# Attention and two routed MLPs: the first block of the second MLP stage gates its last rows on TensorE alone, and the block's steps stand in another order

## The chip, the cores and the metric

The kernel runs on one core of a Trainium2 chip. TensorE (PE) multiplies matrices and transposes tiles; VectorE (DVE), ScalarE (ACT) and GpSimd (POOL) work element by element; SyncE (SP), ACT and POOL issue transfers. The metric is the device time of one launch in microseconds (us).

## What is computed

Inputs: q, k, v of 4 batches x 8 heads x 576 positions x 64, and the weights of two expert stages with N = 2304 rows, D = 512, E = 8 experts, F = 1024.

```python
x = attention_with_rope(q, k, v)                  # 2304 x 512
# first expert stage
logits = x @ w_gate + modality_bias[modality_id]
e = argmax(logits); g = softmax(logits)[e]
x = g * (relu(x @ w1[e]) @ w2[e])
# second expert stage
out = x.copy()
rows = x @ w_skip > 0
e = argmax(x[rows] @ w_gate2); g = softmax(x[rows] @ w_gate2)[e]
out[rows] = x[rows] + g * (relu(x[rows] @ w1_2[e]) @ w2_2[e])
```

## The kernel before

Attention runs first, then the first expert stage (`moe1`) in blocks of 256 rows, each of one expert, then the second (`moe2`) in blocks of 128 rows. Rows get to their expert through lists in DRAM: a row's gate is worked out, its place in its expert's list counted, its number and gate value scattered to the list by an indirect DMA of POOL (`list<-tgs,si`, one issue for 128 rows); a block loads its list, gathers its rows (`xh<-out_dram,tok`), computes, and scatters the result (`out_dram<-x,tok`).

Matrix products work on fp32 values split in a high and a low part, three products for each. ACT casts the high parts of weights and activations (L1000 for w1, L1013 for w2, L1097 for x, L1452 for the hidden rows hT), and DVE subtracts for the low parts (L1004, L1016, L1101, L1453). Blocks 0 to 3 of the second stage belong to the expert with the most rows; on this input ten blocks (0 to 9) run, and during blocks 3 to 8 the weights of the next block's expert are split: four pieces of w1 and eight chunks of w2.

A block of the second stage (`body(i)` in `moe2`) consists of these steps: `mm1(hf, ...)` multiplies the rows with half hf of w1 (L1434), 12 matmuls for a half; `relu(hf)` on ACT (L1444) takes the result out of PSUM; `h_tr(hf)` transposes it on PE (L1449) and splits it into hT (ACT L1452, then DVE L1453); `mm2` multiplies hT with w2 (L1474), 24 matmuls; `xt(i + 1)` turns and splits the next block's rows (L1094, L1097, L1101); `split1` and `split2` split weights for the next block. At the end DVE makes the result (L1532) and POOL scatters it. Every engine works its own instructions off in the order in which the code writes them, so the order of steps in `body` is the order in each queue; `mm1` of the next block needs xT and the w1 pieces, `mm2` needs hT and the w2 chunks.

What is still to be done for the first stage's last 256 rows (its tiles t = 0 and t = 1 of 128 rows) stands in block 0 of the second stage, as calls `last(t, stage)`: `out` scales the rows out of PSUM on ACT (L1183, into tile `x20` or `x21`); the second gate's nine columns (eight experts and the skip score) are then worked out; `top` takes the best expert; `count` and `list` find the place and scatter the list entry. The gate has two ways. For t = 0 before, POOL multiplies x20 with three gate columns (`prod`, L1190, in `moe1`), ACT sums them (`sums`, L1195) and DVE multiplies and sums the six others (L1199). For t = 1, `turn` transposes the rows on PE (L1206), copies them to SBUF on ACT (L1208) and scatters the rows to `out`; `gate` is four matmuls with nine columns (L1213). The tiles `x20` and `x21` are also the source of scatters by POOL's queue. The `prod` tiles are two buffers of `x2t` and the tile `prod`; `relu` and `turn` take their result tiles from the same pool `x2t`.

The functions in the listing keep the line numbers of the profile.

Of the kernel before, what the change touches and what calls it, by code (L numbers as in the profile page):

```python
# [112 lines left out]
class Kernel:  # L113
# [1016 lines left out]
    def moe1(self):  # L1130
# [37 lines left out]
        def epi(i, t, stage):  # L1168
# [5 lines left out]
            if stage == "meta":  # L1174
# [3 lines left out]
                    s[name] = self.rot(f"{name}_{t}", [128, w], dt, bufs=1)  # L1178
                nc.scalar.copy(s["tg"], l[:, t])
                nc.scalar.copy(s["ti"], l[:, t, 0:1])  # L1180
            elif stage == "out":
                s["x2"] = self.rot(f"x2{t}", [128, DM], bufs=1)
                nc.scalar.activation(s["x2"], s["y"], AF.Copy, scale=s["tg"][:, 1:2])  # L1183
            elif stage == "prod":


                s["prod"] = [self.rot("x2t", [128, 4, 128]).rearrange("p c t -> p (c t)") for _ in range(3)][0:2]
                s["prod"].append(self.rot("prod", [128, DM], bufs=1))
                for j, w in enumerate(s["prod"]):
                    nc.gpsimd.tensor_tensor(w, s["x2"], self.gw[j], op=ALU.mult)  # L1190
                    if j == 0:
                        self.scatter(self.out, s["ti"], s["x2"], N)
            elif stage == "sums":
                for j, w in enumerate(s["prod"]):
                    nc.scalar.activation(w, w, AF.Copy, accum_out=s["lg"][:, j : j + 1])  # L1195
            elif isinstance(stage, tuple):

                for e in stage:
                    nc.vector.scalar_tensor_tensor(  # L1199
                        self.junk, s["y"], s["tg"][:, 1:2], self.gw[e], op0=ALU.mult, op1=ALU.mult, accum_out=s["lg"][:, e : e + 1]  # L1200
                    )
            elif stage == "turn":
                x2 = s["x2"]
                ps = self.bank("T")
                for dc in range(4):
                    nc.tensor.transpose(ps[:, dc * 128 : dc * 128 + 128], x2[:, dc * 128 : dc * 128 + 128], self.ident)  # L1206
                s["x2t"] = self.rot("x2t", [128, 4, 128], F32)
                nc.scalar.copy(s["x2t"].rearrange("p c t -> p (c t)"), ps)  # L1208
                self.scatter(self.out, s["ti"], x2, N)
            elif stage == "gate":  # L1210
                pg = self.bank("G")
                for dc in range(4):
                    nc.tensor.matmul(pg[:, 0 : E + 1], s["x2t"][:, dc], self.wg2s[:, dc], start=dc == 0, stop=dc == 3)  # L1213
                nc.vector.tensor_copy(s["lg"], pg[:, 0 : E + 1])
            elif stage == "top":
                v = s["v"]
                lg, nm, d = s["lg"], tl_("nm", [128, 1]), tl_("d", [128, E])
                nc.vector.tensor_reduce(nm, lg[:, 0:E], axis=AX.X, op=ALU.max, negate=True)
                nc.vector.tensor_scalar(d, lg[:, 0:E], nm, None, op0=ALU.add)
                ex = tl_("ex", [128, E])  # L1220
                s["se"] = self.rot("se", [128, 1], F32, bufs=3)
                nc.scalar.activation(ex, d, AF.Exp, accum_out=s["se"])
                t8, m8 = tl_("t8", [128, E]), tl_("m8", [128, 1])
                nc.vector.scalar_tensor_tensor(t8, d, 0.0, self.w8, op0=ALU.is_equal, op1=ALU.mult)
                nc.vector.tensor_reduce(m8, t8, axis=AX.X, op=ALU.max)
                nc.vector.tensor_scalar(v[:, 0:1], s["tg"][:, 0:1], float(N), None, op0=ALU.is_lt)
                nc.vector.tensor_scalar(v[:, 1:2], lg[:, E : E + 1], 0.0, v[:, 0:1], op0=ALU.is_gt, op1=ALU.mult)
                nc.vector.tensor_tensor(m8, m8, v[:, 1:2], op=ALU.mult)
                s["oh"] = self.rot("oh", [128, E], BF16)
                nc.vector.tensor_scalar(s["oh"], self.w8, m8, None, op0=ALU.is_equal)  # L1230
            elif stage == "count":
                pr = s["pr"] = self.bank("G")
                nc.tensor.matmul(pr[:, 0:E], self.U, s["oh"], start=True, stop=False)
                nc.tensor.matmul(pr[:, 0:E], self.ones, self.acc2, start=False, stop=True)
            else:
                v, oh = s["v"], s["oh"]
                nc.vector.tensor_scalar(s["se"], s["se"], 1e-9, None, op0=ALU.add)
                tg = self.rot("tgs", [128, 2], bufs=4)
                nc.vector.reciprocal(tg[:, 1:2], s["se"])
                nc.scalar.copy(tg[:, 0:1], s["tg"][:, 0:1])  # L1240
                sl, sf, si = tl_("sl", [128, E]), tl_("sf", [128, 1]), self.rot("si", [128, 1], I32, bufs=3)
                nc.vector.tensor_tensor(sl, s["pr"][:, 0:E], self.ebase, op=ALU.add)
                nc.vector.tensor_tensor(sl, sl, oh, op=ALU.mult)
                nc.vector.tensor_tensor(self.acc2, self.acc2, oh, op=ALU.add)
                nc.vector.tensor_reduce(sf, sl, axis=AX.X, op=ALU.add)
                nc.vector.tensor_scalar(v[:, 2:3], v[:, 1:2], float(-BIG), float(BIG), op0=ALU.mult, op1=ALU.add)
                nc.vector.tensor_tensor(si, sf, v[:, 2:3], op=ALU.add)
                self.scatter(self.lists[1], si, tg, E * CAP)
                del eps[i, t]
# [159 lines left out]
    def moe2(self):  # L1409
# [14 lines left out]
        def body(i):  # L1424
# [48 lines left out]
                    for hi, wi in ((0, 0), (0, 1), (1, 0)):  # L1473
                        nc.tensor.matmul(y, hT[:, hi, f], w2s[:, wi, f], start=(f == 0 and hi + wi == 0), stop=(f == 7 and hi == 1))  # L1474

            last(1, "out")
            last(0, "sums", (3, 4, 5), (6, 7, 8))
            mm1(0, range(0, 1))
            last(1, "turn")
            if i == 0:  # L1480
                self.moe2_second()
            mm1(0, range(1, 2))
            last(0, "top")
            if i == 0:
                split2(0, range(0, 4))
            split2(i, range(4, 8))
            if i + 2 > NA2 + 1:
                self.seq_load(q, i + 2, 1)
            mm1(0, range(2, 4))
            relu(0)  # L1490
            last(0, "count", "list")
            last(1, "gate", "top")
            mm1(1, range(0, 2))
            h_tr(0)
            split1((0,))
            mm1(1, range(2, 4))
            split1((1,))
            relu(1)
            last(1, "count")
            if i > 0:  # L1500
                fetch(i + 2)
            if i + 3 > NA2:
                self.seq_list(q, i + 3)
            mm2(range(0, 2))
            last(1, "list")
            if i == 0:

                for j in range(NE2, NA2):
                    self.seq_list(q, j)
            h_tr(1)  # L1510
            split1((2, 3))
            if i + 3 > NA2 + 1:
                self.seq_load(q, i + 3, 0)
            mm2(range(2, 4))
            if i == 1:
                tot = self.counts(self.acc2, "d")
            xt(i + 1)
            mm2(range(4, 8))
            if i == 1:

# [81 lines left out]
```

## Time and profile before

| | before |
|---|---|
| median of 3 runs | 750.29 us (750.17 to 752.8) |
| profiled execution | 752.11 us |
| its span on the core | 750.5 us |
| mean granted TensorE clock | 0.979 |

The profile comes from one execution, whose own time is 752.11 us, 1.6 us over its span. Times in the rows are microseconds from the span's start. A timeline row reads: start, busy time, engine, line, operation, result<-inputs, shape, number of instructions of the group, and in brackets the engine's idle time ahead of it with what ended it. In a windows row the busy time of each engine in the stretch stands with its count of instructions.

### The profile page before, as it was taken

What the parts mean: (1) busy time and instruction counts of PE and PEld (TensorE: products, weight loads), DVE (VectorE), ACT (ScalarE), POOL (GpSimd) and SP (SyncE); (2) the same over time, 40 slices, a digit from 0 to 9 for tenths busy, and PEclk for the clock granted to TensorE, in tenths of its full rate; (3) what the DMA queues carried; (4) which work ended last, traced back from release to release, by engine and by line L of the source; (5) the groups of instructions that cost most, each with busy time, mean ns of one, the idle gap of its engine ahead of it and who ended that gap; (6) DMA issues with size and microseconds to landing.
All of it is one profiled execution on the core that took longest, in us unless ns stands there. A gap on an engine that the chain in (4) does not pass through costs nothing. (4 is left out here: it accounts for less than half of the span.)

```text
span 750.5 us, 15355 instructions
## 1 busy us (share of the span) xinstructions
PE 709.6 (95%) x4844; PEld 643.2 (86%) x4844; DVE 548.4 (73%) x1335; ACT 458.2 (61%) x1046; POOL 376.3 (50%) x464
## 2 busy tenths in 40 slices
PE   6899999999999999978999999999998969999995
PEld 6799999999999999978989988998897748777773
DVE  6789999999999999974436544655569773489892
ACT  3788888888888888881223332333255452387881
POOL 7755576759587855244244554254355312123233
PEclk9899999999999999998999999999999989999998
DMA  5665556555656554470411110110677031679910
GB/s 141 129 156 140 127 127 149 130 125 131 155 129 141 137 133 92 103 239 0 128 58 58 57 43 29 43 57 16 170 266 234 22 118 39 249 250 326 331 48 18
DMA packets 76656, 94.68 MB, mean 126 GB/s; under 512 B 29736, under 2 KB 50472, under 8 KB 76547
## 3 DMA queue, kind: packets, MB, share of 16 engines
q1 hardware_dynamic: 67970, 78.22, 37.5%
q0 software_dynamic: 7200, 12.46, 5.3%
q10 hardware_dynamic: 1376, 2.75, 1.1%
q8 instruction: 43, 0.70, 0.4%
q14 instruction: 67, 0.54, 0.3%
HBM read 64.48 MB, written 12.97 MB: 103 GB/s over the span
## 5 line engine op out<-in xcount | busy, mean ns | idle before, releaser
L430 PE MATMUL S<-w1s 128*128 128x288 f32 x640 | 134.1, 323 | 4.0 <-ACT w1s L386 1.3
L1164 PE MATMUL psY<-w2s,hT 128*128 128x512 f32 x480 | 116.0, 396 | 0.0
L1115 PE MATMUL psM<-xT,w1s 128*128 128x256 f32 x864 | 110.6, 286 | 2.6 <-DVE hT L1128 2.6
L1115 PEld LDWEIGHTS psM<-xT,w1s 128*128 128x128 f32 x864 | 106.5, 191 | 3.7 <-DVE hT L1128 3.1
L430 PEld LDWEIGHTS S<-w1s 128*128 128x128 f32 x640 | 98.7, 192 | 8.8 <-ACT PP L447 1.7
L1164 PEld LDWEIGHTS psY<-w2s,hT 128*128 128x128 f32 x480 | 87.9, 188 | 17.3
L447 ACT ACTIVATE PP<-S,nm 128x576 f32<-128x576 f32 x128 | 95.8, 749 | 6.5 <-DVE nm L443 4.4
L443 DVE TENSOR_REDUCE nm<-S 128x1 f32<-128x576 f32 x128 | 94.8, 750 | 3.8 <-PE S L430 3.7
L532 DVE TENSOR_TENSOR tl<-T,th 128x512 fp32r<-128x512 f32 x128 | 88.0, 687 | 12.7 <-ACT th L528 9.4
L525 PE MATMUL T<-ident,PP 128*128 128x128 f32 x512 | 94.3, 274 | 0.8 <-DVE w1s L399 0.4
L528 ACT CAST th<-T 128x512 fp32r<-128x512 f32 x128 | 75.1, 587 | 17.8 <-PE T L525 15.2
L559 PE MATMUL O<-th,vh 128*128 128x288 f32 x256 | 76.4, 332 | 0.9 <-ACT os L568 0.9
L525 PEld LDWEIGHTS T<-ident,PP 128*128 128x128 f32 x512 | 63.9, 140 | 3.4 <-DVE tl L532 1.0
L559 PE MATMUL O<-tl,vh 128*128 128x288 f32 x256 | 64.5, 305 | 0.0
L1434 PE MATMUL psM<-w1s,xT 128*128 128x512 f32 x240 | 63.0, 408 | 1.0 <-DVEq L1351 0.7
L1474 PE MATMUL psY<-w2s,hT 128*128 128x512 f32 x240 | 62.2, 401 | 0.0
L962 POOL DMA_INDIRECT list<-tgs,si x20 | 21.5, 1076 | 80.0 <-issue 40.4
L330 POOL TENSOR_TENSOR mem_w<-qkn,mem_w 128x640 f32<-128x640 f32 x30 | 46.8, 1561 | 20.4 <-PE T L367 20.2
L1128 DVE SCALAR_TENSOR_TENSOR hT<-psM,hT 128x512 fp32r<-128x512 f32 x36 | 24.8, 688 | 43.1 <-ACT hT L1123 43.1
L1434 PEld LDWEIGHTS psM<-w1s,xT 128*128 128x128 f32 x240 | 44.7, 192 | 12.7 <-DVE xT L1101 2.2
L1183 ACT ACTIVATE x<-psY,tg 128x512 f32<-128x512 f32 x20 | 13.8, 689 | 67.7 <-PE psY L1164 56.4
L1101 DVE TENSOR_TENSOR xT<-psT,xT 128x512 fp32r<-128x512 f32 x31 | 20.4, 686 | 44.2 <-ACT xT L1097 43.1
(276 smaller groups left out, 1522.6 us busy)
## 6 DMA issues: line engine op xcount, KB each, us to landing
raw<-in_moe_w_dram SPq DMA_DIRECT2D x24, 512.0 KB
mem_w<-in_moe_w_dram SPq DMA_DIRECT2D x20, 512.0 KB
w1s<-w1s SPq DMA_DIRECT2D x30, 256.0 KB
raw1b<-in_moe_w_dram SPq DMA_DIRECT2D x12, 512.0 KB
raw2b<-in_moe_w_dram SPq DMA_DIRECT2D x12, 512.0 KB
w1s<-w1s SPq DMA_DIRECT2D x16, 288.0 KB
qkn<-in_q_dram SPq DMA_DIRECT2D x16, 256.0 KB
qkn<-in_k_dram SPq DMA_DIRECT2D x16, 256.0 KB
```

The source lines that it names most:

```text
L330: eng.tensor_tensor(r, x, tb[:, i, 0].unsqueeze(1).broadcast_to([128, 2, 5, D]), op=ALU.mult)
L430: yield nc.tensor.matmul(ps[:, hf, 0:288], s["wide"][:, o : o + 128], s["K"][h % 2][:, kk, hf * 288 : hf * 288 + 288], start=first and kk ...
L443: nc.vector.tensor_reduce(st[h // 2]["nm"][:, h % 2, c : c + 1], hs[h]["ps", c][:, :, 0:288], axis=AX.XY, op=ALU.max, negate=True)
L447: nc.scalar.activation(PP[:, c, h % 2 * S : h % 2 * S + S].rearrange("p (a b) -> p a b", a=2), hs[h]["ps", c][:, :, 0:288], AF.Exp, bias=s ...
L525: yield nc.tensor.transpose(ps[:, c * 128 : c * 128 + 128], PP[:, c, o : o + 128], ident)
L528: nc.scalar.copy(hs[h]["th"][:, j, 0:512], hs[h]["tp", j])
L532: nc.vector.tensor_tensor(s["tl"][:, j, 0:512], s["tp", j], s["th"][:, j, 0:512].bitcast(F32), op=ALU.subtract)
L559: yield nc.tensor.matmul(s["ot"][:, hf, 0:288], st[h // 2]["vh"][:, h % 2, j].rearrange("p s d -> p (s d)"), w[:, hf * 288 : hf * 288 + 28 ...
L1115: self.nc.tensor.matmul(ps[:, a], self.w1s[:, wi, dc, fs], x[:, xi, dc], start=(dc == 0 and wi + xi == 0), stop=(dc == 3 and wi == 1))
L1164: nc.tensor.matmul(ps, h[:, hi, f, t * 128 : t * 128 + 128], w2s[:, wi, f], start=(f == 0 and hi + wi == 0), stop=(f == 7 and hi == 1))
L1434: nc.tensor.matmul(ms[hf], x[:, xi, dc], w1s[:, wi, dc, hf * 512 : hf * 512 + 512], start=(dc == 0 and wi + xi == 0), stop=(dc == 3 and xi ...
L1474: nc.tensor.matmul(y, hT[:, hi, f], w2s[:, wi, f], start=(f == 0 and hi + wi == 0), stop=(f == 7 and hi == 1))
```

## The change

The last rows of t = 0 get their gate on PE too: a stage `turn only` (the transposition and the copy, without the scatter, which POOL has issued already) and `gate` take the place of the three sums on ACT and the six products on DVE. POOL's three products stay in `moe1`'s body; nothing reads them now. The rows of t = 1 are scaled into a tile of their own, `x2l`, where before it was `x21`. The steps of `body` stand in another order: in block 0, w2 is split in three parts, and gate, count and list stand elsewhere; in every block `relu(1)` and its half of `mm1` stand ahead of `split1`'s first piece, the second piece behind `h_tr(1)`, and the third and fourth, with the load of w1 that follows them, behind `xt(i + 1)`.

```diff
--- before.py
+++ after.py
@@ -1178,8 +1178,9 @@
                     s[name] = self.rot(f"{name}_{t}", [128, w], dt, bufs=1)
                 nc.scalar.copy(s["tg"], l[:, t])
                 nc.scalar.copy(s["ti"], l[:, t, 0:1])
-            elif stage == "out":
-                s["x2"] = self.rot(f"x2{t}", [128, DM], bufs=1)
+            elif stage in ("out", "last out"):
+
+                s["x2"] = self.rot(f"x2{t}" if stage == "out" else "x2l", [128, DM], bufs=1)
                 nc.scalar.activation(s["x2"], s["y"], AF.Copy, scale=s["tg"][:, 1:2])
             elif stage == "prod":
 
@@ -1199,14 +1200,15 @@
                     nc.vector.scalar_tensor_tensor(
                         self.junk, s["y"], s["tg"][:, 1:2], self.gw[e], op0=ALU.mult, op1=ALU.mult, accum_out=s["lg"][:, e : e + 1]
                     )
-            elif stage == "turn":
+            elif stage in ("turn", "turn only"):
                 x2 = s["x2"]
                 ps = self.bank("T")
                 for dc in range(4):
                     nc.tensor.transpose(ps[:, dc * 128 : dc * 128 + 128], x2[:, dc * 128 : dc * 128 + 128], self.ident)
                 s["x2t"] = self.rot("x2t", [128, 4, 128], F32)
                 nc.scalar.copy(s["x2t"].rearrange("p c t -> p (c t)"), ps)
-                self.scatter(self.out, s["ti"], x2, N)
+                if stage == "turn":
+                    self.scatter(self.out, s["ti"], x2, N)
             elif stage == "gate":
                 pg = self.bank("G")
                 for dc in range(4):
@@ -1473,48 +1475,54 @@
                     for hi, wi in ((0, 0), (0, 1), (1, 0)):
                         nc.tensor.matmul(y, hT[:, hi, f], w2s[:, wi, f], start=(f == 0 and hi + wi == 0), stop=(f == 7 and hi == 1))
 
-            last(1, "out")
-            last(0, "sums", (3, 4, 5), (6, 7, 8))
+
+            last(0, "turn only")
+            last(1, "last out")
             mm1(0, range(0, 1))
             last(1, "turn")
             if i == 0:
                 self.moe2_second()
+            last(0, "gate", "top")
             mm1(0, range(1, 2))
-            last(0, "top")
             if i == 0:
-                split2(0, range(0, 4))
-            split2(i, range(4, 8))
-            if i + 2 > NA2 + 1:
-                self.seq_load(q, i + 2, 1)
+                split2(0, range(0, 2))
+            else:
+                split2(i, range(4, 8))
+                if i + 2 > NA2 + 1:
+                    self.seq_load(q, i + 2, 1)
+            last(1, "gate", "top")
             mm1(0, range(2, 4))
             relu(0)
-            last(0, "count", "list")
-            last(1, "gate", "top")
             mm1(1, range(0, 2))
+            last(0, "count")
             h_tr(0)
+            last(0, "list")
+            mm1(1, range(2, 4))
+            relu(1)
+            if i == 0:
+                split2(0, range(2, 4))
             split1((0,))
-            mm1(1, range(2, 4))
-            split1((1,))
-            relu(1)
-            last(1, "count")
             if i > 0:
                 fetch(i + 2)
             if i + 3 > NA2:
                 self.seq_list(q, i + 3)
             mm2(range(0, 2))
+            last(1, "count")
+            h_tr(1)
+            split1((1,))
             last(1, "list")
             if i == 0:
+                split2(0, range(4, 8))
 
                 for j in range(NE2, NA2):
                     self.seq_list(q, j)
-            h_tr(1)
-            split1((2, 3))
-            if i + 3 > NA2 + 1:
-                self.seq_load(q, i + 3, 0)
             mm2(range(2, 4))
             if i == 1:
                 tot = self.counts(self.acc2, "d")
             xt(i + 1)
+            split1((2, 3))
+            if i + 3 > NA2 + 1:
+                self.seq_load(q, i + 3, 0)
             mm2(range(4, 8))
             if i == 1:
```

ACT's queue at the start of block 0, before, with what each row waits for (L1351 is the last instruction of the first stage; DMASW are the counters of POOL's indirect transfers, one for each of eight queues; names with _49 are the counters of engines):

```order
L1183 ACTIVATE x_0_5294<-psY_5149,tg_0_5203 128x512 [waits DMASW3_49,DMASW2_49,DMASW5_49,DMASW1_49,DMASW6_49,DMASW0_49,DMASW7_49,PE_49,Activation_49]
L1195 ACTIVATE x2t_5133,lg_0_5176<-x2t_5133 128x512 [waits DVE_49,Pool_49]
L1195 ACTIVATE x2t_5132,lg_0_5176<-x2t_5132 128x512 [waits Pool_49]
L1195 ACTIVATE prod_5575,lg_0_5176<-prod_5575 128x512 [waits Pool_49]
L1208 COPY x2t_5132<-psT_5183 128x512 [waits PE_49,Activation_49]
L1222 ACTIVATE e_ex_5380,se_5383<-e_d_5376 128x8 [waits DVE_49]
L1013 CAST w2s<-raw2b 128x512 [waits DMAHW6_49]
```

And of the change:

```order
L1209 COPY x2t_5132<-psT_5183 128x512 [waits DVE_49,PE_49,Pool_49]
L1184 ACTIVATE x2l_10903<-psY_5149,tg_0_5203 128x512 [waits Activation_49]
L1209 COPY x2t_5133<-psT_5182 128x512 [waits PE_49]
L1224 ACTIVATE e_ex_5380,se_5383<-e_d_5376 128x8 [waits DVE_49]
L1013 CAST w2s<-raw2b 128x512 [waits DMAHW6_49]
L1224 ACTIVATE e_ex_5381,se_5384<-e_d_5377 128x8 [waits DVE_49]
L1446 ACTIVATE x2t_5132<-psM_5307 128x512 [waits PE_49,Activation_49]
```

The scaled rows of t = 1 wait for nothing but ACT itself now, and stand behind the copy of the turned rows of t = 0, which waits for a count of POOL's.

PE's queue at the same place, before (psM is the result of mm1, psT of a transposition, psG of the gate; x_0_5294 are the rows of t = 1):

```order
L1434 MATMUL psM_5307<-w1s,xT_5124 128x512 [waits DVE_49,Activation_49]
L1434 MATMUL psM_5307<-w1s,xT_5124 128x512 [waits DVE_49]
L1434 MATMUL psM_5307<-w1s,xT_5124 128x512
L1206 MATMUL psT_5183<-ident,x_0_5294 128x128 [waits Activation_49]
L1206 MATMUL psT_5183<-ident,x_0_5294 128x128 x3
L1434 MATMUL psM_5307<-w1s,xT_5124 128x512 x9
...
L1213 MATMUL psG_5126<-wg2s,x2t_5132 128x9 [waits Activation_49]
L1213 MATMUL psG_5126<-wg2s,x2t_5132 128x9 x3
```

And of the change (x_0_5180 are the rows of t = 0):

```order
L1207 MATMUL psT_5183<-ident,x_0_5180 128x128 [waits DVE_49,Activation_49]
L1207 MATMUL psT_5183<-ident,x_0_5180 128x128 x3
L1436 MATMUL psM_5307<-w1s,xT_5124 128x512 [waits DVE_49] x2
L1436 MATMUL psM_5307<-w1s,xT_5124 128x512
L1207 MATMUL psT_5182<-ident,x2l_10903 128x128 [waits Activation_49]
L1207 MATMUL psT_5182<-ident,x2l_10903 128x128 x3
L1215 MATMUL psG_5127<-wg2s,x2t_5132 128x9 x4
L1436 MATMUL psM_5307<-w1s,xT_5124 128x512 x3
L1215 MATMUL psG_5126<-wg2s,x2t_5133 128x9 [waits DVE_49,Activation_49]
L1215 MATMUL psG_5126<-wg2s,x2t_5133 128x9 x3
```

Four transpositions and four gate matmuls have come in, and the transposition of t = 1 still stands behind the first three matmuls of mm1.

ACT's queue in a block behind which the expert changes, from relu(0) to the w2 casts, before (branches left out; raw_70 and raw2b are loaded weights):

```order
L1444 ACTIVATE x2t_5133<-psM_5307 128x512
L1452 CAST hT<-psT_5182 128x4x128
...
L1000 CAST w1s<-raw_70 128x4x256
...
L1000 CAST w1s<-raw_70 128x4x256
...
L1444 ACTIVATE x2t_5132<-psM_5308 128x512
L1452 CAST hT<-psT_5183 128x4x128
...
L1000 CAST w1s<-raw_70 128x4x256 x2
...
L1097 CAST xT_4883<-psT_5182 128x4x128
...
L1013 CAST w2s<-raw2b 128x512 x4
```

And of the change:

```order
L1446 ACTIVATE x2t_5132<-psM_5307 128x512
L1454 CAST hT<-psT_5183 128x4x128
L1446 ACTIVATE x2t_5133<-psM_5308 128x512
...
L1000 CAST w1s<-raw_70 128x4x256
...
L1454 CAST hT<-psT_5182 128x4x128
...
L1000 CAST w1s<-raw_70 128x4x256
...
L1097 CAST xT_4883<-psT_5183 128x4x128
...
L1000 CAST w1s<-raw_70 128x4x256 x2
...
L1013 CAST w2s<-raw2b 128x512 x4
```

The second relu (to x2t_5132 before, x2t_5133 now) has moved ahead of the four w1 casts, and the w1 casts stand one piece further on each: behind relu(1), behind hT of the second half, and behind xT.

## Rows read from the trace of the kernel before

**Rows 1.** The page's first part: busy time, share and instructions of PE.

```profile
PE 709.6 (95%) x4844; PEld 643.2 (86%) x4844; DVE 548.4 (73%) x1335; ACT 458.2 (61%) x1046; POOL 376.3 (50%) x464
```

**Rows 2.** Windows by block of the second stage: block 0, 2, 3 to 8, 9.

```profile
core 0: us, PE busy (x) PEld busy (x) DVE busy (x) ACT busy (x) POOL busy (x), PEclk, DMA share, GB/s
599.41:623.17 23.76, 16.42 (x76) 12.63 (x77) 15.93 (x56) 10.54 (x27) 5.90 (x6) 0.86 0.29 102
...
635.68:648.12 12.44, 12.44 (x62) 10.18 (x60) 7.11 (x26) 2.96 (x5) 1.80 (x3) 1.00 0.44 142
648.12:728.30 80.18, 76.92 (x361) 60.05 (x360) 67.46 (x87) 62.07 (x96) 22.30 (x26) 1.00 0.74 260
728.30:741.35 13.05, 12.92 (x61) 9.85 (x59) 8.16 (x14) 6.27 (x12) 4.84 (x4) 1.00 0.02 2
```

**Rows 3.** Timeline of all engines where the second stage begins.

```profile
599.41 0.93 PE L1434 MATMUL psM<-w1s,xT 128*128 128x512 f32 x3 [0.72 <-DVEq L1351]
...
600.56 1.27 POOL L1190 TENSOR_TENSOR prod<-x,raw1b 128x512 f32<-128x512 f32 x1
...
601.90 2.26 SPq L1036 DMA_DIRECT2D raw1b<-in_moe_w_dram  x4
...
604.76 0.69 ACT L1183 ACTIVATE x<-psY,tg 128x512 f32<-128x512 f32 x1 [10.50 <-DMA out_dram<-x,ti]
...
605.50 1.11 PE L1206 MATMUL psT<-ident,x 128*128 128x128 f32 x4 [5.16 <-ACT x L1183]
```

**Rows 4.** Windows of block 0, columns as in group 2.

```profile
602.00:602.25 0.25, 0.00 (x0) 0.00 (x0) 0.21 (x3) 0.00 (x0) 0.00 (x0) 0.91 0.00 0
602.25:605.50 3.25, 0.00 (x0) 0.00 (x1) 2.15 (x6) 0.74 (x2) 0.00 (x0) 0.50 0.75 252
605.50:609.00 3.50, 3.50 (x11) 2.91 (x12) 1.40 (x9) 3.48 (x11) 1.00 (x1) 0.50 0.96 345
...
614.85:616.50 1.65, 0.00 (x0) 0.00 (x0) 1.41 (x9) 1.16 (x4) 0.97 (x1) 1.00 0.02 5
```

**Rows 5.** Timeline of PE later in block 0.

```profile
609.78 1.04 PE L1213 MATMUL psG<-wg2s,x2t 128*128 128x9 f32 x8
...
616.55 0.17 PE L1233 MATMUL psG<-oh,U 128*128 128x8 bf16 x1 [1.73 <-DVE oh L1230]
```

**Rows 6.** Timeline: from block 0's lists to the rows of block 2.

```profile
615.53 0.98 POOL L962 DMA_INDIRECT list<-tgs,si  x1 [8.72 <-issue]
...
620.24 0.97 POOL L962 DMA_INDIRECT list<-tgs,si  x1 [3.73 <-DVE hT L1453]
...
624.47 1.01 POOL L962 DMA_INDIRECT out_dram<-x,tok  x1 [0.32 <-DVE x L1532]
...
628.05 1.06 POOL L952 DMA_INDIRECT xh<-out_dram,tok  x1 [2.37 <-DMA out_dram<-x,tok]
...
632.46 0.64 PE L1094 MATMUL psT<-ident,xh 128*128 128x128 f32 x4
```

**Rows 7.** DMA issues in 627 to 628.9 us: count, median us to landing.

```profile
xh<-out_dram,tok POOLq DMA_INDIRECT x1, 3.6
```

**Rows 8.** Timeline of ACT over one block in which the expert changes.

```profile
677.69 0.60 ACT L1444 ACTIVATE x2t<-psM 128x512 f32<-128x512 f32 x1 [0.25 <-PE psM L1434]
679.52 0.59 ACT L1452 CAST hT<-psT 128x512 fp32r<-128x512 f32 x1 [1.23 <-PE psT L1449]
680.26 2.00 ACT L1000 CAST w1s<-raw1b 128x1024 fp32r<-128x1024 f32 x2 [0.15 <-DMA raw<-in_moe_w_dram]
682.16 0.59 ACT L1444 ACTIVATE x2t<-psM 128x512 f32<-128x512 f32 x1
683.54 0.59 ACT L1452 CAST hT<-psT 128x512 fp32r<-128x512 f32 x1 [0.79 <-ACT x2t L1444]
...
686.66 4.26 ACT L1013 CAST w2s<-mem_w 128x512 fp32r<-128x512 f32 x8
691.07 0.60 ACT L1444 ACTIVATE x2t<-psM 128x512 f32<-128x512 f32 x1 [0.15 <-issue]
```

**Rows 9.** Timeline of PE in the same block, its only wait.

```profile
682.80 0.66 PE L1449 MATMUL psT<-ident,x2t 128*128 128x128 f32 x4 [0.56 <-ACT x2t L1444]
```

**Rows 10.** Timeline of DVE in the same block.

```profile
688.24 2.48 DVE L1016 TENSOR_TENSOR w2s<-mem_w,w2s 128x512 fp32r<-128x512 f32 x4
```

## The prediction

> **What bounds the kernel now.** I read the page first: PE is busy 95% of the span [rows 1], so the time can fall only where PE idles or runs at half clock. The windows by block show where that is in the second stage. Block 0 takes 23.76 us with 16.42 us of PE work at a mean clock of 0.86; block 2, which splits no weights, runs without a gap in 12.44; the six blocks 3 to 8, each followed by another expert's weights, take 80.18 us, 13.36 each, of which PE idles 3.26 in all; the last takes 13.05 [rows 2]. So there is something to win in block 0 (7.34 us of idle) and some 0.9 us in each of the six.
>
> The timeline of block 0 says what PE waits for. Its first three matmuls end at 600.34, and the next thing in its queue, the transposition of t = 1's scaled rows, starts at 605.50, because ACT scales them only at 604.76; ACT has idled 10.50 us by then, with a scatter of POOL's as the releaser [rows 3]. The order lists it: that scaling waits for the counters of seven of POOL's transfer queues. The windows show what this costs beside the gap: the clock leaves full speed (2.4 GHz) at about 602.2, after 1.9 us without work, and is at half (1.2 GHz) until 609.0, that is for 3.5 us after work has come back [rows 4]. A later gap, the count of t = 1 waiting 1.73 us for its one-hot row [rows 5], leaves the clock at 1.00 [rows 4].
>
> In the six blocks I read ACT's timeline: from one relu(0) to the next are 13.38 us, and what lies between is a queue with small gaps (0.25, 1.23, 0.15, 0.79, 0.15) [rows 8]. PE's one gap in the block, 0.56 us, is the transposition of the second half, which waits for relu(1); that relu stands behind two w1 casts of 2.00 us together [rows 8, 9].
>
> **Block 0: the gate of t = 0 on PE, the tile x2l.** Removed are three sums on ACT and six products on DVE; both lie in the stretch in which PE waits for something else, and are worth nothing by themselves. x2l takes the wait for the seven transfer queues away. But ACT's queue now has the copy of t = 0's turned rows ahead of it, and that copy waits for a count of POOL's. The copy writes a buffer of the pool in which POOL's products lie, and these still run. The last product ends at 600.56 + 1.27 = 601.83, and SP's load into the weights' buffer goes out at 601.90 [rows 3]; I take the copy to start there too, at 601.9. The scaling follows some 0.55 later (an ACT instruction of that shape is busy 0.59 [rows 8]), and PE's transposition 0.74 behind the scaling's start (604.76 to 605.50 before), so at about 603.2: 2.3 us earlier, not 5.
>
> From there to block 1 PE had 15.49 us of work (16.42 less the first 0.93) and 2.18 of idle (7.34 less 5.16). The work grows by the gate of t = 0: its four transpositions lie in the gap and cost nothing there (0.66 of it [rows 9]); its gate costs what the gate of t = 1 shows, 1.04 busy, 0.89 until the next matmul starts [rows 5]. Of the idle, the 1.73 goes, since the count of t = 1 now stands behind the first chunks of mm2 with its top worked out long before; I leave 0.45 for relu and the w2 splits, which are late by turns. Does the clock still fall? PE idles from about 600.95 to 603.2, 2.25 us: longer than the 1.9 after which it fell and the 1.73 through which it stayed. So I take half clock, for 3.5 us as before. Block 1 then starts at 603.2 + 15.49 + 0.89 + 0.45 = 620.0 instead of 623.17: **-3.2**. Bounds: if the clock stays up, the 3.5 us at half [rows 4] shrink by at most 1.75, of which I take 1.2, as part of the stretch is waiting: -4.4; if all 2.18 us of idle come back in another place (the w2 chunks now arrive in three lots, and each lot is waited for), 621.8, -1.4.
>
> The Trainium skill ("TensorE: Matmul & The Clock Gate", section "Wait — 56ns, not 53.3ns?") has a floor of about 25 ns from start to start for small matmuls. By it the eight recorded gate matmuls would take 0.2 us in place of the 0.89 measured here, and the sum would be 0.7 lower; the row disagrees, and it decides.
>
> **What comes early because of it: block 2's rows.** Block 2's rows are gathered on POOL behind a chain: list scatter of t = 0 at 615.53, of t = 1 at 620.24 (4.71 later), loads of lists, the scatter of block 0's result at 624.47, the gather at 628.05 [rows 6], which lands 3.6 us later [rows 7], at 631.65. PE takes the rows at 632.46 [rows 6], 0.8 us after. If block 1 starts 3.2 earlier, PE wants them at 629.3. The list of t = 0 stands on DVE behind hT's low part, and I put its scatter at 614.0, 1.5 earlier; with 4.71 to t = 1 and everything else behind it as before, the gather lands at about 630.1. So PE waits 0 to 0.85; I take **+0.6**, near the upper end, since the intervals are measured ones.
>
> The Trainium skill ("DMA: Bandwidth & Descriptors", section "Anatomy of one DMA — SWDGE (gpsimd) path") gives a fixed 2.0 us for a transfer of this kind; if the second list followed the first by that, the gather would be in time and the sum 0.6 lower. The row shows 4.71 between the two.
>
> **Blocks 3 to 9: relu(1) ahead of the w1 casts.** It takes away what PE waits for at the second transposition, but moves 4 us of w1 casts to later places in ACT's queue, where they push the w2 casts, and behind these the next block's relu(0). I follow ACT's queue with the durations of [rows 8], from relu(0) at 0. hT of the first half starts at 1.3 (if PE waits for the relu) to 1.8 (as before, 677.69 to 679.52). relu(1) needs six more matmuls and ends at 3.3 to 3.7. Then a w1 cast (to 4.3 to 4.7), hT of the second half, which waits for PE's transposition behind six matmuls of mm2 (to 5.3 to 5.9), the second w1 cast (to 6.4 to 6.9), xT, which waits for six more matmuls and a transposition (to 7.1 to 7.7), the last two w1 casts (to 9.2 to 9.6), the eight w2 casts of 4.26 (to 13.5 to 13.9), and relu(0) again. The gap that the w1 casts filled, ahead of relu(1), is now empty; that is why the round gets no shorter though a wait of PE's is gone. DVE decides between the ends: its w2 low parts, 2.48 for four [rows 10], stand ahead of the low part of hT, for which mm2 waits. It is busy 67.46 of 80.18 us [rows 2], so I take the upper, 13.9.
>
> Block 3 has no w2 casts ahead of its own relu(0), and wins: 12.6, near the 12.44 of block 2. Blocks 4 to 8 take 13.9 each. Block 9 splits nothing but begins behind the last w2 casts: 13.05 and the 0.6 by which its relu(0) is later, 13.7. Together 12.6 + 69.5 + 13.7 = 95.8 against 80.18 + 13.05 = 93.23: **+2.6**. Bounds: with 13.5 a block, 12.44 + 67.5 + 13.05 = 93.0, -0.2; with another 0.5 a block from DVE, 14.4, it is 12.6 + 72.0 + 14.1 = 98.7, +5.5. The load of w1 that moved behind the last two casts waits for their buffer anyway; that its weights come in time I take from the casts, which wait 0.15 us at most in their idle for a transfer [rows 8].
>
> **Sum.** -3.2 + 0.6 + 2.6 = 0.0. The profiled execution took 752.11 us, 1.6 over its span of 750.5, and would take that again; it lies 1.8 above the median of 750.29, and I put the change on the median: **750.3 us**. A measurement of this kernel can tell about 0.5%, 3.75 us, from no change.
>
> **Rivals.**
> 1. Faster: nothing new is waited for in the six blocks. relu(1) ahead of the casts takes PE's idle of 3.26 us away and relu(0) is not pushed, because the casts catch up in ACT's idle (2.6 us a block in [rows 8]). With -3.2 in block 0, and the gather in time, that is -6.5: 743.8. For it: ACT is busy only 62.07 of 80.18 us [rows 2]. Against it: those gaps are ACT waiting for PE at places that stay.
> 2. Slower: the low parts on DVE become the bound. hT's low part waits behind w2's eight low parts, mm2 behind it, and the next casts behind mm2's transpositions; a round then takes about 14.6. 12.6 + 73.0 + 14.3 = 99.9, +6.7, with -3.2 and 0.6 in all +4.1: 754.4. It decides from about 14.5 a block on. For it: DVE has only 2.1 us a block to spare. Against it: the w1 low parts come later now, not earlier, and DVE's work has not grown.
> 3. The change doesn't do what it says: the count that the copy waits for comes not with POOL's product but only when POOL has waited for its own transfers, near 604.4, just ahead of where ACT began before (604.76). Then the copy stands ahead of the scaling for nothing, block 0 gains only the 1.73 less the gate's 0.89 and some of the sums, about 1, and the time is 752.5.
>
> **How the numbers follow.** Forecast 0.58, rival 1 0.17, rival 2 0.13, rival 3 0.12. Rival 3 and the forecast lie within 0.5%: faster 0.17, same 0.70, slower 0.13. The forecast with its bounds (-4.4 to -1.4, 0 to 0.85, -0.2 to +5.5) spans 746 to 755 at the extremes, seldom together; leaving out most of rival 1 and half of rival 2 gives a range of 745.5 to 754.5.
>
> **What would show it.** In block 0: ACT's copy at about 601.9 and the transposition of x2l at 603.2 (604.5 or later is rival 3), the clock at 0.50 for some 3.5 us behind it, block 1's first matmul at 620, and PE waiting for a gather at block 2's xt. In blocks 4 to 8: no PE gap at the second transposition, but one at the first, waiting for a relu(0) that stands behind w2 casts, and 13.9 us from relu(0) to relu(0). The forecast is wrong if that round is under 13.4, or if the matmuls of mm2 wait for low parts of hT by more than a few tenths.

## The result and the profile after

The changed kernel took 757.2 us (median of 4 runs, 756.49 to 758.07) beside 751.54 for the kernel before on the same chip: a ratio of 1.0078, 95% interval 1.0056 to 1.01. It is slower, and the prediction's 750.3 us, with its range to 754.5, is missed. A longer comparison (12 runs beside 28 of before, below) gave 1.0041, 1.0024 to 1.0058.

The windows by block of the changed kernel: block 0, block 1, blocks 3 to 8, block 9, with the columns of [rows 2].

```profile
600.24:623.58 23.34, 20.09 (x88) 16.30 (x89) 11.89 (x45) 9.53 (x22) 5.72 (x5) 0.78 0.30 104
623.58:637.10 13.52, 12.71 (x62) 10.21 (x61) 3.91 (x10) 3.12 (x6) 4.62 (x7) 1.00 0.17 56
649.54:731.28 81.74, 77.14 (x361) 60.35 (x360) 66.33 (x87) 62.15 (x94) 27.82 (x26) 1.00 0.70 254
731.28:745.37 14.09, 13.11 (x61) 9.85 (x59) 9.19 (x14) 7.19 (x14) 4.84 (x4) 1.00 0.02 2
```

Block 1 of before, which stands between the first two rows of [rows 2]:

```profile
623.17:635.68 12.51, 12.51 (x62) 10.13 (x61) 3.89 (x10) 3.13 (x6) 4.09 (x7) 1.00 0.18 59
```

Block 0 takes 23.34 us where it took 23.76, block 1 13.52 where it took 12.51, the six blocks 81.74 where they took 80.18, the last 14.09 where it took 13.05. So block 0 gave 0.4 us, block 1 took 1.0, and blocks 3 to 9 took 2.6 (95.83 against 93.23).

The timeline at the start of the second stage answers to [rows 3], all of it 0.83 us later in this execution.

```profile
601.42 1.27 POOL L1191 TENSOR_TENSOR prod<-x,raw1b 128x512 f32<-128x512 f32 x1
...
602.77 0.58 ACT L1209 COPY x2t<-psT 128x512 f32<-128x512 f32 x1 [7.64 <-POOLq L1353]
603.25 0.69 ACT L1184 ACTIVATE x2l<-psY,tg 128x512 f32<-128x512 f32 x1
603.99 1.11 PE L1207 MATMUL psT<-ident,x2l 128*128 128x128 f32 x4 [2.43 <-ACT x2l L1184]
604.90 1.71 PE L1215 MATMUL psG<-wg2s,x2t 128*128 128x9 f32 x8
...
609.45 4.64 PE L1436 MATMUL psM<-w1s,xT 128*128 128x512 f32 x12
...
633.84 0.66 PE L1094 MATMUL psT<-ident,xh 128*128 128x128 f32 x4 [0.81 <-DMA xh<-out_dram,tok]
```

The copy starts as POOL's last product ends, and the transposition of t = 1's rows follows 1.2 us behind it, at 603.99: 2.3 us earlier than before, counted from the stage's start. But eight gate rows take 1.71 instead of 1.04 [rows 5], and twelve matmuls of mm1 take 4.64. The last row is block 2's rows: PE waits 0.81 for their gather. The clock (the first figure behind POOL's busy time) in windows of the same stretch, for [rows 4]:

```profile
602.50:602.75 0.25, 0.00 (x0) 0.00 (x0) 0.00 (x0) 0.00 (x0) 0.18 (x1) 0.98 0.00 0
602.75:603.99 1.24, 0.00 (x0) 0.00 (x0) 0.00 (x0) 1.17 (x2) 0.00 (x0) 0.50 0.39 40
603.99:612.75 8.76, 8.76 (x31) 7.79 (x32) 4.45 (x20) 2.50 (x8) 1.00 (x1) 0.50 0.64 237
612.75:613.00 0.25, 0.25 (x2) 0.17 (x1) 0.00 (x0) 0.25 (x1) 0.00 (x0) 0.54 0.00 0
```

Work comes back at 603.99, and the clock is at half until about 613.0, 9.0 us later. Before, it was back at full 3.5 us after the work.

In the later blocks, ACT from one relu(0) to the next, for [rows 8]:

```profile
680.10 0.58 ACT L1446 ACTIVATE x2t<-psM 128x512 f32<-128x512 f32 x1
681.48 0.59 ACT L1454 CAST hT<-psT 128x512 fp32r<-128x512 f32 x1 [0.79 <-ACT x2t L1446]
682.89 0.60 ACT L1446 ACTIVATE x2t<-psM 128x512 f32<-128x512 f32 x1 [0.82 <-PE psM L1436]
683.63 1.05 ACT L1000 CAST w1s<-raw1b 128x1024 fp32r<-128x1024 f32 x1
685.32 0.59 ACT L1454 CAST hT<-psT 128x512 fp32r<-128x512 f32 x1 [0.64 <-PE psT L1451]
686.29 1.05 ACT L1000 CAST w1s<-raw1b 128x1024 fp32r<-128x1024 f32 x1 [0.38 <-DMA raw2b<-in_moe_w_dram]
687.25 0.58 ACT L1097 CAST xT<-psT 128x512 fp32r<-128x512 f32 x1
687.84 2.00 ACT L1000 CAST w1s<-raw1b 128x1024 fp32r<-128x1024 f32 x2
689.74 4.26 ACT L1013 CAST w2s<-mem_w 128x512 fp32r<-128x512 f32 x8
693.91 0.58 ACT L1446 ACTIVATE x2t<-psM 128x512 f32<-128x512 f32 x1
```

The round takes 13.81 us here (13.38 before). ACT now waits 0.82 ahead of relu(1), where two casts stood, 0.64 ahead of the second hT, and the last two w1 casts run only behind xT; w2's casts follow, and relu(0) behind them. PE feels it at the first transposition and in mm2:

```profile
694.55 0.66 PE L1451 MATMUL psT<-ident,x2t 128*128 128x128 f32 x4 [0.52 <-ACT x2t L1446]
...
697.65 1.19 PE L1476 MATMUL psY<-w2s,hT 128*128 128x512 f32 x4 [0.58 <-DVE hT L1455]
```

and DVE's rows name the second wait: four low parts of w2 stand ahead of the low part of hT.

```profile
694.51 2.48 DVE L1016 TENSOR_TENSOR w2s<-mem_w,w2s 128x512 fp32r<-128x512 f32 x4
696.92 0.67 DVE L1455 TENSOR_TENSOR hT<-psT,hT 128x512 fp32r<-128x512 f32 x1
```

### The profile page after: what moved, and what is told of

It reads as the page before. It is cut to its first block, busy times and chain, and to the rows that moved or that the text cites. A ratio compares the mean times of both kernels' runs of the same rounds, so it can differ in the third digit from the quotient of the medians.

```text
span 754.8 us, 15358 instructions
## 1 busy us (share of the span) xinstructions
PE 715.0 (95%) x4856; PEld 648.2 (86%) x4856; DVE 544.2 (72%) x1324; ACT 458.3 (61%) x1041; POOL 381.3 (51%) x464
## 3 DMA queue, kind: packets, MB, share of 16 engines
q10 hardware_dynamic: 1376, 2.75, 1.1%
## 5 line engine op out<-in xcount | busy, mean ns | idle before, releaser
L1164 PE MATMUL psY<-w2s,hT 128*128 128x512 f32 x480 | 116.1, 396 | 0.0
L1164 PEld LDWEIGHTS psY<-w2s,hT 128*128 128x128 f32 x480 | 87.9, 188 | 17.3
L447 ACT ACTIVATE PP<-S,nm 128x576 f32<-128x576 f32 x128 | 95.8, 749 | 6.5 <-DVE nm L443 4.4
L532 DVE TENSOR_TENSOR tl<-T,th 128x512 fp32r<-128x512 f32 x128 | 88.0, 687 | 12.7 <-ACT th L528 9.1
L1476 PE MATMUL psY<-w2s,hT 128*128 128x512 f32 x240 | 63.9, 403 | 3.2 <-DVE hT L1455 1.9
L330 POOL TENSOR_TENSOR mem_w<-qkn,mem_w 128x640 f32<-128x640 f32 x30 | 46.9, 1563 | 20.6 <-PE T L367 20.4
L1476 PEld LDWEIGHTS psY<-w2s,hT 128*128 128x128 f32 x240 | 43.1, 188 | 14.4 <-DVE hT L1455 4.1
L1436 PEld LDWEIGHTS psM<-w1s,xT 128*128 128x128 f32 x240 | 45.8, 195 | 10.1
L334 POOL TENSOR_TENSOR mem_w<-qkn,mem_w 128x320 f32<-128x320 f32 x60 | 51.0, 873 | 0.0
```

Of the source, the lines that this page charges most:

```text
L334: eng.tensor_tensor(t2r[:, :, :, a : a + 32], x[:, :, :, o : o + 32], sn, op=ALU.mult)
L447: nc.scalar.activation(PP[:, c, h % 2 * S : h % 2 * S + S].rearrange("p (a b) -> p a b", a=2), hs[h]["ps", c][:, :, 0:288], AF.Exp, bias=s ...
L532: nc.vector.tensor_tensor(s["tl"][:, j, 0:512], s["tp", j], s["th"][:, j, 0:512].bitcast(F32), op=ALU.subtract)
L1164: nc.tensor.matmul(ps, h[:, hi, f, t * 128 : t * 128 + 128], w2s[:, wi, f], start=(f == 0 and hi + wi == 0), stop=(f == 7 and hi == 1))
L1436: nc.tensor.matmul(ms[hf], x[:, xi, dc], w1s[:, wi, dc, hf * 512 : hf * 512 + 512], start=(dc == 0 and wi + xi == 0), stop=(dc == 3 and xi ...
```

## The experiments

Ratios are to the kernel before, run on the same chip; "blocks" are read from each kernel's own profile.

**1. The steps of before in blocks 1 to 9.** Block 0 stays changed.

```diff
             last(0, "list")
+            if i > 0:
+                split1((0,))
             mm1(1, range(2, 4))
+            if i > 0:
+                split1((1,))
             relu(1)
...
             h_tr(1)
-            split1((1,))
+            if i == 0:
+                split1((1,))
+            else:
+                split1((2, 3))
...
```

> The changed kernel with the steps of blocks 1 to 9 in the order of before; block 0 stays changed. If the new place of the w1 casts is what costs in blocks 3 to 9 (95.8 us there in the changed kernel against 93.2), these blocks come back to about 93.2 and the time falls by 2.6 us against the changed kernel, to about 0.4% over before. Rival: the later blocks are slow because block 0 hands them its lists and rows late, whatever their own order: then they stay at 95 to 96 and the time does not move.

1.001 (0.999 to 1.003). Blocks 3 to 9 took 94.0 us, of which PE waits 0.95 for one late gather in block 7; without it they are at before's 93.2. So the order in these blocks is what costs there, not the early block 0. Block 0, the same instructions as in the changed kernel, took 22.25, with 6.8 us at half clock where the changed kernel's profile has 10.2. The windows in which the clock falls and comes back:

```profile
598.50:598.75 0.25, 0.25 (x4) 0.25 (x3) 0.00 (x0) 0.25 (x1) 0.00 (x0) 0.78 1.09 377
605.25:605.50 0.25, 0.25 (x2) 0.15 (x2) 0.00 (x0) 0.23 (x1) 0.00 (x0) 0.57 0.04 16
```

Work had come back at 597.66, so the clock fell 1.0 us after it, and was back at full 7.8 us after it.

**2. Block 0 of before, the new order of relu(1) and the casts.**

> The other half alone: block 0 with the gate, the tile and the steps of before, relu(1) ahead of the casts in all blocks. If the two parts add, block 0 takes 23.8, block 1 12.5 with no wait for the gather, blocks 3 to 9 95.8: 2.6 us over before (0.35%). Rival: the two parts touch, and without the early block 0 the later blocks lose less or more than 2.6.

1.004 (1.0021 to 1.0059), 3.0 us; block 0 23.73, block 1 12.51 without a wait, blocks 3 to 9 95.74. By the blocks the parts add: +0.4 in run 1 and +2.5 here, against +3.2 for the whole change.

**3. The gates behind the first half of mm1.**

```diff
-            last(0, "gate", "top")
             mm1(0, range(1, 2))
...
-            last(1, "gate", "top")
             mm1(0, range(2, 4))
+            last(0, "gate", "top")
             relu(0)
+            last(1, "gate", "top")
```

> The changed kernel with both gates moved behind the first half of mm1, so that after the transposition of t = 1 nine matmuls of mm1 follow one another, as before. If the small gate matmuls between them kept the clock at half for 9.0 us, it is back some 3.5 us after that transposition, and block 0 takes 20.5 to 21.5 us in place of 23.3. Rival: the half clock has the same length whatever stands there, or block 0's time is set by the three lots of w2 chunks: block 0 stays within 0.5 of 23.3.

Block 0 and the clock in it:

```profile
597.74:618.01 20.27, 17.24 (x88) 13.81 (x89) 11.75 (x45) 9.43 (x22) 5.60 (x5) 0.92 0.35 119
601.29:604.00 2.71, 2.71 (x9) 2.32 (x10) 0.43 (x1) 1.56 (x3) 0.03 (x1) 0.50 0.90 328
604.00:604.25 0.25, 0.25 (x2) 0.24 (x1) 0.25 (x2) 0.06 (x1) 0.25 (x1) 0.63 0.65 262
```

With work from 601.29 on and no gate amid it, the clock is back at 604.2, 2.9 us later, and block 0 takes 20.27 us: 3.1 under the changed kernel, and what the prediction had put on block 0 (620.0 less 599.41, 20.6). The three lots of w2 chunks are the same in both. One profile shows this. The mean granted clock of the whole span, which does not say where the clock fell, fits it in the other executions: it is 0.983 to 0.985 in eight of this run's twelve, and at most 0.981 in the twelve of run 5, the changed kernel. (6.8 us less at half clock, of 750, would raise that mean by 0.0045, an estimate.)

The whole time does not show the gain as clearly: it ran at 1.0036 (1.0013 to 1.0059), 2.7 us over before, where the profile's blocks give +0.2 (block 0 -3.5, block 1 +1.0, blocks 3 to 9 +2.7). The interval reaches down to +1.0. Three executions have a mean clock of 0.975 and take 754 to 756 us; what executions differ by elsewhere is told at the end.

**4. x2l ahead of the copy on ACT.**

```diff
-            last(0, "turn only")
             last(1, "last out")
+            last(0, "turn only")
```

> The changed kernel with one step turned round: ACT scales the rows of t = 1 ahead of the copy that waits for POOL. PE's gap then shrinks from 2.4 to about 1.2 us, the clock should stay at full, and the gates and matmuls run at full: block 0 about 18 to 19 us in place of 23.3. The list chain on POOL does not shorten by as much, so block 2's gather should be waited for by some 3 us, and of the 5 won 2 to 3 should stay. Rival: the clock falls all the same, and block 0 gains only the 1.2 us of the gap.

0.9991 (0.9972 to 1.001), block 0 in 18.00 us with no half clock, block 1 in 13.04. PE waits 0.32 for block 2's gather, not the 3 that were expected, because the first list scatter came earlier too: 12.1 us into block 0, where it was 16.1 before. On PE the gates now cost what [rows 5] had:

```profile
598.51 0.60 PE L1207 MATMUL psT<-ident,x2l 128*128 128x128 f32 x4
600.08 1.06 PE L1215 MATMUL psG<-wg2s,x2t 128*128 128x9 f32 x8 [0.96 <-ACT x2t L1209]
600.99 0.95 PE L1436 MATMUL psM<-w1s,xT 128*128 128x512 f32 x3
601.77 0.96 PE L1215 MATMUL psG<-wg2s,x2t 128*128 128x9 f32 x8
```

The gap is now 0.96, ahead of the gate. Against the changed kernel (run 5, 1.0041) the ratios show 3.7 of the 5.3 us won in block 0.

**5. The changed kernel again.**

> The changed kernel itself once more. The blocks of the first two profiles account for 3.2 us over before (block 0 -0.4, block 1 +1.0, blocks 3 to 9 +2.6), while the medians of four runs stood 5.7 apart. If the blocks tell the whole effect, a longer comparison gives about 3 us over before (0.4%), and block 0 a half clock of 6.8 to 10.2 us, as its two profiles so far; if the change also costs something outside these blocks, the difference stays at 5 to 6 us (0.7%).

1.0041 (1.0024 to 1.0058), 3.1 us over before: the 3.2 of the first profile's blocks are the whole effect. Block 0 took 23.65 with 10.2 us at half clock, blocks 3 to 9 96.1.

**6. The first w1 piece back ahead of relu(1).**

> The changed kernel with one step put back: the first w1 piece ahead of the second half of mm1 and so of relu(1); the other three pieces stay late. If blocks 4 to 8 are slow because ACT stands empty ahead of relu(1) and makes up for it behind xT, the cast fills that gap again and a round takes 12.9 to 13.3 us instead of 13.6 to 14.1: 3 to 5 us less. Rival: the round is set by DVE, hT's low part behind the w2 low parts (mm2 waits 0.34 for it in each block): then it stays at 13.6 or more.

A miss: 1.0035 (1.0019 to 1.0051), rounds of 13.6 to 14.1 as in the changed kernel, blocks 3 to 9 95.8. ACT has no gap ahead of relu(1) any more, and waits 1.57 us ahead of the second hT instead. "The gap ahead of relu(1)" as the sole cause falls. The rival, a round set by hT's low part, keeps its forecast here: in each block mm2 still waits 0.34 to 0.48 us.

**7. Runs 1 and 4 together.**

> Both mends together: x2l ahead of the copy, and blocks 1 to 9 in the order of before. If the parts add, block 0 takes 18.0 us, block 1 13.0 with its wait for the gather, blocks 3 to 9 93.2 to 94.0: 4.5 to 5.2 us under before, 0.65%. Rival: an earlier block 0 only moves the wait to the gathers of the later blocks, and less than 3 us is left.

0.9952 (0.9934 to 0.997), 3.6 us under before, less than expected; block 0 18.24, block 1 13.47, blocks 3 to 9 93.15.

**8. relu(1) between the first two pieces.** As run 7, with

```diff
-            if i > 0:
-                split1((1,))
             relu(1)
+            if i > 0:
+                split1((1,))
```

> As e7, with relu(1) of blocks 1 to 9 between the first and the second w1 piece (before: behind both; changed kernel: ahead of both). ACT then has a cast to do while relu(1) waits for PE, and PE has its second transposition without waiting: the wait of 0.4 to 0.6 us a block goes, a round takes 12.8 to 13.1 us, and 2 to 3 us more than e7 are won. Rival: DVE's low parts or the gathers take the place of the wait, and the round stays at 13.3.

0.9924 (0.9894 to 0.9954). Rounds of 12.4 to 12.9, blocks 3 to 9 88.5 where before has 93.2: the wait of [rows 9] is gone and no other has come in these blocks. The blocks of this profile, the fastest of six executions, are 9.5 us under before's; the ratio gives 5.7. Where the other executions lose the rest is not shown.

**9. The last two pieces back ahead of xt, in the changed kernel.**

> The changed kernel with the third and fourth w1 piece back ahead of xt; relu(1) stays ahead of all casts. The run with the first piece put back left the round at 13.6 to 14.1, and ACT now waited 1.6 us ahead of the second hT instead of 0.8 ahead of relu(1): so a single gap is not the cause. New theory: ACT has three waits for PE in a round (ahead of relu(1), of the second hT, of xT), and each w1 cast that does not stand in one of them delays the w2 casts and relu(0). Here the wait ahead of xT gets its casts back and the one ahead of relu(1) stays empty: 13.2 to 13.5, between the changed kernel and before. Rival: what matters is only that both first pieces stand ahead of the second hT; then this run stays at 13.6 to 14.1.

1.006 (1.0042 to 1.0078), rounds of 13.7 to 13.9: the round did not move, but the wait did. PE now waits at the start of the next block's mm1,

```profile
684.37 0.73 PE L1436 MATMUL psM<-w1s,xT 128*128 128x512 f32 x2
686.13 4.00 PE L1436 MATMUL psM<-w1s,xT 128*128 128x512 f32 x16 [1.03 <-DVE xT L1101]
```

for xT's low part, which DVE makes behind three w1 low parts in a row:

```profile
681.98 3.50 DVE L1004 TENSOR_TENSOR w1s<-raw1b,w1s 128x1024 fp32r<-128x1024 f32 x3 [0.34 <-ACT w1s L1000]
685.39 0.68 DVE L1101 TENSOR_TENSOR xT<-psT,xT 128x512 fp32r<-128x512 f32 x1
```

So the expected number was wrong; the rival's, 13.6 to 14.1, came, but it names no such wait either.

**10. The last two pieces behind xt, in the kernel of run 8.**

> The kernel with relu(1) between the first two casts (a round of 12.4 to 12.9 us there), with the third and fourth piece behind xt as in the changed kernel. By the theory of three waits, the one ahead of xT is empty now and a round grows by 0.6 to 1.2 us, to 13.2 to 13.8. Rival: the place of the last two pieces is free, and the round stays at 12.6.

0.9993 (0.9972 to 1.0014); rounds of 13.65 to 14.1 where run 8 has 12.4 to 12.9. This one move gives the whole loss. ACT stands empty ahead of xT,

```profile
678.06 0.59 ACT L1454 CAST hT<-psT 128x512 fp32r<-128x512 f32 x1 [0.63 <-PE psT L1451]
679.85 0.59 ACT L1097 CAST xT<-psT 128x512 fp32r<-128x512 f32 x1 [1.19 <-PE psT L1094]
680.57 2.00 ACT L1000 CAST w1s<-raw1b 128x1024 fp32r<-128x1024 f32 x2
```

and PE waits where it does in the changed kernel: for relu(0), then for hT's low part.

```profile
673.48 0.66 PE L1451 MATMUL psT<-ident,x2t 128*128 128x128 f32 x4 [0.77 <-ACT x2t L1446]
...
676.35 1.20 PE L1476 MATMUL psY<-w2s,hT 128*128 128x512 f32 x4 [0.36 <-DVE hT L1455]
```

Block 0, which is that of run 4, took 21.19 here: the clock fell behind the first gates, 0.9 us after work had come back (windows: the block, the gates of t = 0, the half clock):

```profile
595.12:616.31 21.19, 19.12 (x88) 15.37 (x89) 11.66 (x45) 8.96 (x22) 5.83 (x5) 0.84 0.33 114
598.14:599.00 0.86, 0.86 (x8) 0.86 (x8) 0.00 (x0) 0.44 (x1) 0.00 (x0) 1.00 0.63 100
599.25:605.75 6.50, 6.50 (x20) 5.44 (x21) 4.22 (x20) 2.23 (x7) 1.26 (x1) 0.50 0.83 304
```

**11. The kernel before with one line moved: relu(1) ahead of the second piece.**

> The kernel before with one line moved: relu(1) ahead of the second w1 piece, nothing else. If the gain of blocks 3 to 9 in the combined kernel (88.5 against 93.2 us) comes from this line alone, block 0 stays at 23.8, block 1 at 12.5 and blocks 3 to 9 take 88.5: 4.7 us under before, 0.63%. Rival: the early rows and lists of the mended block 0 have a share in it, and 2 us or more are missing.

0.9963 (0.9947 to 0.998), 2.8 us under before, where 4.7 was expected. Blocks 3 to 9 took 90.3. Block 7 (14.54) is 1.9 us longer than the others, since PE waits 1.57 there for a late gather; the other rounds are 12.4 to 12.7, as in run 8. So the line gives the gain of these blocks, but whether the mended block 0 has a share in the gather's being in time stays open.

**12. Runs 3, 4 and 8 together.**

> x2l ahead of the copy, both gates behind the first half of mm1, and relu(1) between the first two w1 pieces in blocks 1 to 9. If PE's gap and the gates amid the first matmuls are what brings the clock down, PE now has nine matmuls of mm1 to do while ACT and POOL get the copies ready: no gap over 1 us, no half clock, block 0 17.5 to 18.5 us, block 1 with a wait for the gather up to 13.5, blocks 3 to 9 88.5 to 90.3 (the latter with one late gather): 7 to 9 us under before by the blocks, about 1%. Rival: the clock falls in this place whatever the order (it did in one of four profiles with x2l ahead), and block 0 takes 21.

0.9913 (0.989 to 0.9936), 6.5 us under before. As in run 8 the blocks of the profile give more, 10.4 us. Block 0, block 1, blocks 3 to 8, block 9:

```profile
598.55:615.43 16.88, 15.84 (x88) 12.77 (x89) 11.56 (x45) 8.87 (x22) 5.84 (x5) 1.00 0.41 143
615.43:629.16 13.73, 12.71 (x63) 10.21 (x62) 3.93 (x10) 3.13 (x6) 4.74 (x8) 1.00 0.17 55
641.59:717.26 75.67, 75.56 (x362) 60.45 (x360) 67.26 (x88) 62.36 (x97) 23.97 (x26) 1.00 0.76 274
717.26:730.13 12.87, 12.87 (x61) 9.86 (x59) 7.98 (x13) 5.98 (x11) 5.14 (x5) 1.00 0.02 2
```

Block 0 is at 16.88 without half clock, and in blocks 3 to 8 PE is busy 75.56 of 75.67 us. What is left is block 1, where the gather is waited for (1.0 us): POOL's chain [rows 6] takes 12.6 us from the first list scatter to the gather, 12.5 before, so it did not shorten with block 0.

## Why the prediction was wrong

- **x2l and the copy: right.** The copy at the end of POOL's product, the transposition 2.3 us earlier, and POOL in the place of the transfer queues came as told; run 4 shows that the copy alone kept the rest of the gap.
- **"So I take half clock, for 3.5 us as before": wrong, and this is the step that failed.** That the clock falls was right. But the changed kernel puts sixteen small gate rows between the transposition behind the gap and the last six matmuls of mm1's first half, and the clock came back 9.0 us after work did (7.8 in run 1), not 3.5. 5.5 us more at half are 2.75 us lost, by an estimate that takes all of PE's work there at double time; that is the miss: block 0 gave 0.4 in place of 3.2. Run 3, which moves the gates alone, has the clock back after 2.9 us and block 0 at 20.27, the 20.6 that was predicted. The other profiles divide the same way: with the gates there, 10.1, 9.9 and 10.3 us after work (runs 5, 6 and 9); with block 0 of before, 5.4 and 4.2 (runs 2 and 11). The bounds (-4.4 to -1.4) had a longer half clock nowhere: the duration was taken from one execution, and from a stretch with other work in it. Why the clock stays down longer behind such rows is not shown.
- **The gate's price: right for full clock only.** 1.04 in [rows 5] and 1.06 in run 4, but 1.71 at half. The floor of 25 ns that the Trainium skill ("TensorE: Matmul & The Clock Gate", section "Wait — 56ns, not 53.3ns?") gives is a lower bound that these rows do not come near: eight take 0.96 to 1.06 us in run 4, and 1.71 at half clock.
- **The gather: right in kind, not in its working.** 0.81 us of wait, block 1 +1.0, against +0.6. But both ends of the sum moved with the longer half clock: the first list scatter went out at 617.74, not 614.0, and block 1 began at 623.58, not 620.0. The two list scatters were 4.59 us apart (4.71 in [rows 6]), and not the 2.0 that the Trainium skill ("DMA: Bandwidth & Descriptors", section "Anatomy of one DMA — SWDGE (gpsimd) path") gives as the fixed cost of one transfer. POOL's idle time between the two, 3.52 us, ended with an instruction of DVE's, so the distance is not shown to be the price of a transfer.
- **Blocks 3 to 9: right.** 95.83 against 95.8, rounds of 13.6 to 14.1 against 13.9, with the waits named: relu(0) behind w2's casts, hT's low part behind w2's low parts. That the sum fits to 0.03 is partly luck: block 9 took 14.09 in place of 13.7, and the others made up for it. Which move is to blame was read too narrowly: it was put on the place ahead of relu(1). Run 10 gives the whole loss with the third and fourth piece behind xt; with these back and relu(1) ahead of all casts (run 9) the loss stays, through xT's low part. Each alone is enough, so neither shows when the other is undone, nor does a lone first piece (run 6).
- **The rivals.** Rival 1 was refuted for this order, but its mechanism holds for another: relu(1) between the pieces takes PE's wait away (runs 8 and 11). Rival 2's forecast of slower came, but not by its mechanism: mm2 does wait for hT's low part, 0.34 to 0.58 us, yet the round stayed near 13.8 and far from 14.6. Rival 3's condition did not occur.
- **The size.** The blocks add up to 3.2 us, as run 5's 3.1. The first comparison's 5.7 us rests on four runs of each kernel. What is left of it, 2.5, is of the size by which executions of the changed kernel differ ahead of the second stage. Run 5's profile, of the same kernel, starts its second stage at 597.55, the first one at 600.24, 2.7 us later, with 10.2 us at half clock at the end of the attention in place of 3.4:

```profile
325.00:365.00 40.00, 35.05 (x233) 31.62 (x232) 22.62 (x53) 16.43 (x33) 15.25 (x31) 0.96 0.31 89
```

The row is run 5's; that of the first profile, with 0.87, stands in the last section. The four runs' mean granted clock is 0.974 to 0.979, that of run 5's twelve 0.979 to 0.981. By run 5's ratio the time would be 753.4, inside the range. So the failed step is 2.8 of the 5.7 us and the gather 0.4; the rest, as far as these rows show, is what executions of one kernel differ by, for which the sum had no term.

## What to carry to other kernels

Put the waiting and the non-waiting work of a shared queue in the order in which they can run: one step turned round on ACT (x2l ahead of the copy) gave block 0 another 5.3 us in the profiles (3.7 in the ratios), where the tile, the gate and the new order had given 0.4. Fill each wait of an in-order engine with a piece of the deferrable work, and count all its waits before moving a piece: three small gaps held four casts in run 8, and each order tried that left one of them open (the changed kernel, runs 6, 9 and 10) lost about a microsecond a block against it. Do not take the length of half clock from one execution as a constant: behind gaps of 2.2 to 2.4 us it lasted 2.9 us from the return of work in run 3, with nine large matmuls first and the gates later, and 7.8 to 10.3 with the gates first.

## What the runs showed of the hardware that was not expected

The length of half clock varied between executions of the same instructions: with the changed block 0 it was 10.2 us in four profiles (the changed kernel's two, runs 6 and 9) and 6.8 in run 1. With block 0 of before it was 6.8 in all three (the kernel before, runs 2 and 11). With x2l ahead of the copy it did not occur in runs 4, 7 and 8, and did in run 10, with a gap of 1.26 us: the same gap as in run 7, and shorter than the 1.42 of run 8. So the gap ahead does not decide alone, and what does is open; in run 12, which has neither the gap nor the gates there, it did not occur.

The same holds for a place that no kernel here changes. Windows of the end of the attention, the changed kernel and run 1:

```profile
325.00:365.00 40.00, 34.80 (x219) 31.65 (x217) 20.30 (x43) 15.57 (x31) 18.55 (x33) 0.87 0.27 80
```

```profile
325.00:365.00 40.00, 35.12 (x242) 31.60 (x241) 23.76 (x64) 16.14 (x32) 14.26 (x29) 1.00 0.34 104
```

A mean clock of 0.87 over 40 us is some 10 us at half in the one execution, and there is none in the other. In the profiles the second stage starts between 594.0 and 600.2 us, with the same program ahead of it. That spread is as large as any effect studied here, which is why blocks were compared, and not spans.
